# Attention of the first token pair in bursts of two tiles, beside the first sub-block's expert passes

## The chip, the cores and the metric

The kernel runs on one core of a Trainium2 chip. The metric is device microseconds of one execution. Before the change the median of three runs is 1481.53 us (1480.02 to 1481.65). Matrix products run on TensorE (PE in the profile); VectorE (DVE), ScalarE (ACT) and GpSimd (POOL) do the elementwise work, and every DMA is issued by SyncE's queue (SP). Each engine works through its own instructions in order and waits on semaphores for the others.

## The reference

Two stages follow one another. First a chunked attention over q, k, v of shape 8 x 8 heads x 576 positions x 64: the sequence is cut into chunks of 64 positions, and each chunk attends only to itself.

```
scores = q_c @ k_c^T / 8                       # 64 x 64 per chunk and head
attn   = exp(scores - max) ; attn /= (sum(attn) + 1e-9)
x      = attn @ v_c                            # back to 4608 tokens x 512
```

Then a dense mixture of four experts over those 4608 tokens, all experts for all tokens:

```
p   = domain_probs / (sum + 1e-9)
out = sum over e of  p[:, e] * (relu(x @ w1[e]) @ w2[e])      # 512 -> 1024 -> 512
```

## The kernel before

**Tiles and passes.** A tile is 128 tokens (two chunks of all eight heads), a sub-block 512 tokens, a pair two sub-blocks (eight tiles). The 4608 tokens are one first sub-block and four pairs. An expert's hidden layer is cut in halves, so each set of tokens needs eight passes, one per expert and half. The products are done in a split form: every fp32 operand is kept as a high and a low part, and each product is the sum of three partial ones (hi-hi, hi-lo, lo-hi).

**The first sub-block** goes through plain passes 0 to 7. Pass 0 is woven into the start-up. Each of passes 1 to 7 (`plain_pass`) is eight steps of 12 partial products each: four hidden steps (`plain_hidden`, f = 0 to 3), whose results go through ReLU on ACT (L721) and a low part on DVE (L722), and four output steps (`Tile.whole`, tiles 0 to 3), whose results DVE adds to the output (L1011). An output step takes its 12 products in the order f = 0 to 3, three for each f; the first six use the first half of the pass's second weights, the last six the second half.

**Weights made beside it.** While these passes run, POOL prepares weights: the low parts of the pass's second weights (`w2_split`, on POOL as L435 `hf<-wf`, `hf<-ws` or `hf<-hf`, four quarters per pass), the low parts of the next pass's first weights (`wf<-wf`), and sums and low parts of factors that later pairs will use (`acc`, `xh`, `xl`). Each low part follows a cast on ACT (L432). So the second half of a pass's output step 0, from its eighth product, needs what POOL finishes last of that pass's four quarters.

**Attention beside it.** The attention of pair 0, the eight tiles that the fast passes start with, is a generator (`attention`) that `Beside.go` moves on by one piece before each step of the plain passes; so its order is written out by hand, and a piece's instructions stand in each engine's queue just before the step's own. A tile takes five pieces: subtract the row maximum (DVE L307, L309) and exponential (ACT L312); row sums, reciprocal and scaling (DVE L315, L316, L318, L322) and a 32x32 block transpose (DVE L188); placing the blocks (ACT L194, L198, five copies); an empty piece; and the burst on PE. A burst before the change is 16 products of 64x64 for the values of the tile that is ready (L208), then 16 for the scores of the next tile (L161), each shown in the trace as two records. Scores and values lie in two halves of one PSUM tile, `psa`, and two ACT copies (L221, L222) take the values to x.

**PSUM banks.** Six banks A0, A1, B0, B1, C0, C1 are given out in rotation by `bank()`. In passes 1 to 6 all eight steps take the next one in turn. In pass 7 the four hidden steps take the next in turn, but the four output tiles have names of their own:

```
o = tiles(0, n, range(NT), ("A1", "B1", "C0", "C1") if last_pass else None)
```

**Later pairs.** Pair 1 uses the one-tile form inside the fast passes (`attend`). Pairs 2 and 3 use a two-tile form (`attend_two`): `two_next` does the values of two tiles (L282, 32 products of 64x64 into the two banks B1 and C1) and the scores of the next two (L263, 32 products into both halves of `psa`) in one burst; the second tile's q and k are loaded into columns of x's own buffer (`xraw`) that are not yet written, and its v into others. `inverse_sums` puts the row sums z into PSUM in all forms.

Of the kernel before, what the change touches and what calls it, by code (L numbers as in the profile page):

```python
# [8 lines left out]
F32 = mybir.dt.float32  # L9
# [22 lines left out]
def chunk_attention_moe(ctx: ExitStack, tc: tile.TileContext, qk, v, v0, dp, w1, w2, out):  # L32
# [33 lines left out]
    def bank(name=None):  # L66
        if name is None:
            name = BANKS[turn[0] % len(BANKS)]
            turn[0] += 1
        return ps.tile([P, SUB], F32, name=name)  # L70
# [47 lines left out]
    def a_load(t):  # L118
        s = st[t] = {}
        s["x"] = load.tile([P, 2, 2, HG, C], F32, name="qk_in")  # L120
        nc.sync.dma_start(out=s["x"], in_=qk[t].rearrange("g c d x h s -> (c d) g x h s"))

    def a_load_v(t, odd=(False, True)):
        s = st[t]
        if not odd[0]:
            s["v"] = load.tile([P, 2 * HG, C], F32, name="v_in")
        to, of = (
            a.rearrange("p (g i h) d -> p g i (h d)", g=2, i=2) for a in (s["v"], v[t - NT])
        )
        if not odd[0]:  # L130
            nc.sync.dma_start(out=to[:, :, 0], in_=of[:, :, 0])
        if odd[-1]:
            for half in range(2):
                rows, other = slice(half * C, (half + 1) * C), slice((1 - half) * C, (2 - half) * C)
                nc.sync.dma_start(out=to[rows, :, 1], in_=of[other, :, 1])

    def a_load_after(t):
        if (t + 1 - NT) % (PAIR * NT):
            a_load(t + 1)
# [23 lines left out]
    def a_less_max(t):  # L163
        less_max(st[t]["sc"])

    def a_exps(t):
        a_exp(st[t]["sc"])
# [9 lines left out]
    def a_scale(t):  # L177

        s = st[t]
        s["e"] = att.tile([P, 2, HG, C], F32, name="e")  # L180
        scale(s["e"], s["sc"], s["r"])
# [5 lines left out]
    def a_transpose(t):  # L187
        nc.vector.transpose(st[t]["sc"], st[t]["e"])  # L188

    def a_place(t, name="pt"):  # L190

        s = st[t]
        s["pt"] = att.tile([P, 2, HG, C], F32, name=name)
        nc.scalar.copy(out=s["pt"], in_=s["sc"])  # L194
        for half in range(2):
            for i in range(2):
                here, there = (slice(half * C + k * B, half * C + (k + 1) * B) for k in (i, 1 - i))
                nc.scalar.copy(  # L198
                    out=s["pt"][there, :, :, i * B : (i + 1) * B],
                    in_=s["sc"][here, :, :, (1 - i) * B : (2 - i) * B],  # L200
                )
# [31 lines left out]
    def two_load(t, i):  # L233
        if i == 0:
            a_load(t)
            return
        pair = (t - NT) // (PAIR * NT)
        to = of_tiles(pair, 6, 2).rearrange("p (g x) (h s) -> p g x h s", x=2, h=HG)
        st[t] = {"x": to}
        for g in range(2):  # L240
            nc.sync.dma_start(out=to[:, g], in_=qk[t, g].rearrange("c d x h s -> (c d) x h s"))

    def two_load_v(t, i, odd):
        if i and not odd:
            pair, j = divmod(t - NT, PAIR * NT)
            st[t]["v"] = of_tiles(pair, 7 if j == 7 else 5, 1).rearrange("p j (h d) -> p j h d", h=2)
        elif not odd:
            st[t]["v"] = load.tile([P, NK, 2, C], F32, name="v_in")
        to = st[t]["v"].rearrange("p (g i) h d -> p g i h d", i=2)
        of = v[t - NT].rearrange("p (g i h) d -> p g i h d", g=2, i=2)  # L250
        if not odd:
            nc.sync.dma_start(out=to[:, :, 0], in_=of[:, :, 0])
            return
        for half in range(2):
            rows, other = slice(half * C, (half + 1) * C), slice((1 - half) * C, (2 - half) * C)
            nc.sync.dma_start(out=to[rows, :, 1], in_=of[other, :, 1])
# [6 lines left out]
            nc.tensor.matmul(s["sc"][of_half(half), c, slot], lhsT=q, rhs=k, start=True, stop=True)  # L263

    def two_sums(t):
        z = bank("B1")[:, : 2 * HG].rearrange("p (c j) -> p c j", c=2)
        st[t]["r"] = inverse_sums(st[t]["sc"], z)

    def two_weights(t):
# [1 line left out]
        a_scale(t)  # L271
        a_transpose(t)

    def two_next(t, scores):

        av = None
        if t is not None:
            av = [bank(name).rearrange("p (i j k) -> p i j k", i=2, k=C) for name in ("B1", "C1")]
            for i in range(2):
                s = st.pop(t + i)  # L280
                for c, half, slot, head in quarters():
                    nc.tensor.matmul(  # L282
                        av[half][of_half(slot % 2), i, head // 2],
                        lhsT=s["v"][of_half(half), head // 2, head % 2],
                        rhs=s["pt"][of_half(half), c, slot], start=True, stop=True,
                    )
        if scores is not None:
            for i in range(2):
                two_scores(scores + i, i)
        if av:  # L290
            pair, j = divmod(t - NT, PAIR * NT)
            to = of_tiles(pair, j, 2).rearrange("p j (i c q) -> p i j c q", i=2, c=2)
            for half in range(2):
                for odd in range(2):
                    nc.scalar.copy(out=to[:, :, odd::2, half ^ odd], in_=av[half][:, :, odd::2])
# [25 lines left out]
    def scale(e, a, r):  # L321
        nc.vector.tensor_tensor(out=e, in0=a, in1=r, op=ALU.mult)  # L322

    def attention(pair, close):

        first = (1 + pair * PAIR) * NT
        last = first + PAIR * NT  # L330
        a_load(first)
        yield
        a_next(None, first)
        for t in range(first, last):

            if close:
                steps = (a_less_max, a_exps), (a_weights, a_transpose), (None, a_place), (None, None)
            else:
                steps = (a_less_max, a_exps), (a_sums, a_scale), (a_transpose, None), (a_place, None)
            for now, then in steps:  # L340
                yield
                if now:
                    now(t)
                if then:
                    deferred.append(lambda then=then: then(t))
            yield
            a_next(t, t + 1 if t + 1 < last else None)

    def a_next(t, after, loads=True):

        if t is not None:
            a_values(t)
        if after is not None:
            a_scores(after)

        if t is not None:
            a_copy(t)
        if loads and after is not None:
            a_load_v(after)
            a_load_after(after)  # L360

# [108 lines left out]
    class Factors:  # L472


        def __init__(self, i, n, places):
            self.i, self.n, self.made = i, n, {}
            self.at = {f"a{f + 1}{k + 1}": raw[i, f, k] for f, k in QUADS}
            self.places = places
# [436 lines left out]
    class Outer:  # L915
# [17 lines left out]
        def add(self, src, i, s):  # L933
            key = self.n // n_pass, 2 * i + self.g + NK * s
            if key not in acc:
                acc[key] = opool.tile([P, SUB], F32, name=f"acc{key[1]}")
                nc.scalar.copy(out=acc[key], in_=src)
            else:
                nc.vector.tensor_tensor(out=acc[key], in0=src, in1=acc[key], op=ALU.add)  # L939
# [337 lines left out]
    class Beside:  # L1277


        def __init__(self, pair, close):  # L1280
            self.steps = attention(pair, close)

        def go(self):
            next(self.steps, None)
# [173 lines left out]
    def loads(at, i, t):  # L1458

        for after, f in enumerate((  # L1460
            lambda: a_load_v(t, (False,)), lambda: a_load_v(t, (True,)), lambda: a_load_after(t),
        )):
            later.append((i + 2 + after, f)) if i + 2 + after >= len(WOVEN) else add(at, i + 2 + after, f)
# [4 lines left out]
    def attend(at, pair, places, i):  # L1468
        t = (1 + pair * PAIR) * NT + i
        after = t + 1 if i + 1 < PAIR * NT else None  # L1470
        if i == 0:
            add(at, 13, lambda: a_next(None, t, False))
            add(at, 14, lambda: a_softmax(t))
            loads(at, 13, t)
        add(at, places[0], lambda: a_weights(t), lambda: a_transpose(t))
        add(at, places[1], lambda: a_place(t))
        add(at, places[2], lambda: a_next(t, after, False))
        if after:
            add(at, places[2] + 1, lambda: a_softmax(after))
            loads(at, places[2], after)  # L1480
# [255 lines left out]
        by_halves(steps["b"])  # L1736

    with tc.manual_schedule():
        beside = Beside(0, True)
        startup(beside)  # L1740
        xs = []
        for n in range(1, n_pass):
            held = plain_pass(n, beside, xs)
        ahead = first_later_pass(n_pass, held)
        for n in range(n_pass + 1, n_run):
            ahead = later_pass(n, *ahead)
        last_products(ahead[0])
# [45 lines left out]
```

## Time and profile before

| quantity | value |
|---|---|
| median of three runs | 1481.53 us |
| profiled execution | 1479.55 us, span 1477.5 us |
| PE busy | 1462.5 us (99%) |
| DVE, ACT, POOL busy | 1076.6 (73%), 623.6 (42%), 980.4 us (66%) |
| DMA engines' mean busy share | 71.5% over the span, 86 to 98% from 44 to 176 us |
| granted PE clock | 1.00 |
| 64x64 products of pair 0 | from 40.8 to 162 us |

How to read it: the page gives one profiled execution. A row of the timeline has the start, the duration, the engine, the kernel line, the operation with what it writes and reads, and how many instructions were merged (x7); in square brackets stands how long the engine was idle before it and what ended that. PE's records are pipelined: in a row of equal products one starts every 0.227 us though each lasts 0.39. A product of the plain passes is one such record.

### The profile page before, as it was taken

What the parts mean: (1) busy time and instruction counts of PE and PEld (TensorE: products, weight loads), DVE (VectorE), ACT (ScalarE), POOL (GpSimd) and SP (SyncE); (2) the same over time, 40 slices, a digit from 0 to 9 for tenths busy, and PEclk for the clock granted to TensorE, in tenths of its full rate; (3) what the DMA queues carried; (4) which work ended last, traced back from release to release, by engine and by line L of the source; (5) the groups of instructions that cost most, each with busy time, mean ns of one, the idle gap of its engine ahead of it and who ended that gap; (6) DMA issues with size and microseconds to landing.
All of it is one profiled execution on the core that took longest, in us unless ns stands there. A gap on an engine that the chain in (4) does not pass through costs nothing.

```text
span 1477.5 us, 23345 instructions
## 1 busy us (share of the span) xinstructions
PE 1462.5 (99%) x8556; PEld 1199.4 (81%) x8556; DVE 1076.6 (73%) x1490; ACT 623.6 (42%) x1165; POOL 980.4 (66%) x730
## 2 busy tenths in 40 slices
PE   8999999999999999999999999999999999999998
PEld 7887877787778788888888888888888888888887
DVE  5566658888887886777766977777668866666665
ACT  4556634544454444444433434444334333333332
POOL 5778888888877785555657656555557655555555
PEclk9999999999999999999999999999999999999999
DMA  8798886878777789766665689676555696665655
GB/s 308 266 335 317 304 299 220 267 232 271 242 244 237 243 260 264 248 216 232 196 213 195 218 228 283 217 242 201 193 205 195 200 255 197 202 206 191 208 189 154
DMA packets 201250, 346.94 MB, mean 235 GB/s; under 512 B 70176, under 2 KB 114480, under 8 KB 200752
## 3 DMA queue, kind: packets, MB, share of 16 engines
q1 hardware_dynamic: 201136, 345.45, 71.5%
q8 instruction: 68, 1.11, 0.3%
q14 instruction: 46, 0.38, 0.1%
HBM read 274.01 MB, written 71.38 MB: 234 GB/s over the span
## 4 chain that ended last, share of the span: by engine, by line
PE 89%; DVE 4%; POOL 3%; issue 1%; DMA 1%; ACT 1%; SPq 0%; POOLq 0%; DVEq 0%; ACTq 0%
PE A L714 47%; PE C L714 26%; PE B L714 13%; POOL hf L435 2%; DVE acc L939 1%; PE psa L208 1%; PE psa L263 1%; PE psa L161 1%; DVE xraw L560 1%; DVE xl L435 1%; POOL wf L435 1%; POOL hf L892 1%; PE B L282 0%; DVE wraw L883 0%; DMA wf<-w 0%
## 5 line engine op out<-in xcount | busy, mean ns | idle before, releaser
L892 POOL TENSOR_TENSOR hf<-wraw,hf 128x512 fp32r<-128x512 f32 x384 | 510.1, 1347 | 222.7 <-ACT hf L889 221.3
L714 PE MATMUL A<-hf,wf 128*128 128x512 f32 x1536 | 392.9, 391 | 3.2 <-POOL hf L892 1.6
L714 PE MATMUL A<-xh,wf 128*128 128x512 f32 (+1 forms) x1104 | 380.5, 388 | 0.0
L889 ACT CAST hf<-wraw 128x512 fp32r<-128x512 f32 x384 | 234.2, 622 | 297.0 <-DVE wraw L883 96.2
L714 PEld LDWEIGHTS A<-hf,wf 128*128 128x128 f32 x1536 | 285.5, 188 | 68.4 <-DVE acc L939 5.9
L714 PEld LDWEIGHTS A<-xh,wf 128*128 128x128 f32 x1104 | 206.7, 188 | 42.9
L777 ACT COPY s<-A 128x512 f32<-128x512 f32 x192 | 112.8, 588 | 291.2 <-PE A L714 290.8
L714 PE MATMUL A<-xl,wf 128*128 128x512 f32 (+1 forms) x552 | 213.7, 388 | 0.0
L939 DVE TENSOR_TENSOR acc<-A,acc 128x512 f32<-128x512 f32 x232 | 158.0, 681 | 71.9 <-PE A L714 71.3
L714 PE MATMUL C<-xh,wf 128*128 128x512 f32 (+1 forms) x600 | 203.5, 386 | 0.7 <-ACT xh L432 0.7
L714 PE MATMUL C<-hf,wf 128*128 128x512 f32 x768 | 195.4, 390 | 1.8 <-DVE acc L939 1.7
L714 PEld LDWEIGHTS C<-hf,wf 128*128 128x128 f32 x768 | 143.8, 188 | 33.2 <-DVE acc L939 2.3
L714 PEld LDWEIGHTS C<-xh,wf 128*128 128x128 f32 x600 | 111.4, 188 | 24.1 <-ACT xh L432 0.8
L883 POOL TENSOR_TENSOR wf<-wraw,wf 128x512 f32<-128x512 f32 x31 | 40.6, 1310 | 128.9 <-DVE wf L877 128.9
L714 PE MATMUL B<-xh,wf 128*128 128x512 f32 (+1 forms) x376 | 125.1, 383 | 0.0
L892 POOL TENSOR_TENSOR hf<-wf,hf 128x512 fp32r<-128x512 f32 x64 | 90.9, 1420 | 48.8 <-ACT hf L889 48.8
L714 PEld LDWEIGHTS A<-xl,wf 128*128 128x128 f32 x552 | 103.5, 188 | 21.2
L939 DVE TENSOR_TENSOR acc<-C,acc 128x512 f32<-128x512 f32 x120 | 82.7, 689 | 45.1 <-PE C L714 42.6
L714 PE MATMUL C<-xl,wf 128*128 128x512 f32 (+1 forms) x300 | 114.5, 385 | 0.0
L883 DVE TENSOR_TENSOR wraw<-wf,wraw 128x512 f32<-128x512 f32 x64 | 95.4, 1491 | 5.2 <-POOL hf L892 4.0
L714 PE MATMUL B<-hf,wf 128*128 128x512 f32 x384 | 97.8, 390 | 0.0
L883 POOL TENSOR_TENSOR wraw<-wraw 128x512 f32<-128x512 f32 x64 | 94.2, 1472 | 0.0
(218 smaller groups left out, 1969.0 us busy)
## 6 DMA issues: line engine op xcount, KB each, us to landing
wf<-w SPq DMA_DIRECT2D x399, 512.0 KB, 4.2
w<-wf SPq DMA_DIRECT2D x49, 512.0 KB, 5.0
w<-hf SPq DMA_DIRECT2D x28, 512.0 KB, 7.4
qk_in<-in_qk SPq DMA_DIRECT2D x24, 512.0 KB, 5.8
w<-hf SPq DMA_DIRECT2D x42, 256.0 KB, 5.1
wf<-in_w SPq DMA_DIRECT2D x19, 512.0 KB, 7.1
ws<-p_t SPq DMA_DIRECT2D x24, 256.0 KB, 3.9
xraw<-in_w SPq DMA_DIRECT2D x24, 256.0 KB, 4.3
```

The source lines that it names most:

```text
L161: nc.tensor.matmul(s["sc"][of_half(half), c, slot], lhsT=q, rhs=k, start=True, stop=True)
L208: nc.tensor.matmul(av[of_half(slot % 2), half, head // 2], lhsT=s["v"][of_half(half), head], rhs=s["pt"][of_half(half), c, slot], start=Tr ...
L263: nc.tensor.matmul(s["sc"][of_half(half), c, slot], lhsT=q, rhs=k, start=True, stop=True)
L435: eng.tensor_tensor(out=t[1], in0=src, in1=t[0].bitcast(F32), op=ALU.subtract)
L560: (eng or nc.vector).tensor_tensor(out=to, in0=a, in1=b, op=op)
L714: nc.tensor.matmul(out, lhsT=lhs(k, a), rhs=rhs(k, b), start=first and i == 0, stop=last and i == len(parts) - 1, skip_group_check=not (fi ...
L777: nc.scalar.copy(out=t, in_=self.a)
L883: (eng or nc.vector).tensor_tensor(out=self.values[place, k], in0=self.values[a, k], in1=self.values[b, k], op=op)
L889: nc.scalar.copy(out=self.part(name, 0)[:, k], in_=self.values[name, k])
L892: (eng or nc.gpsimd).tensor_tensor(out=self.part(name, 1)[:, k], in0=self.values[name, k], in1=self.part(name, 0)[:, k].bitcast(F32), op=A ...
L939: nc.vector.tensor_tensor(out=acc[key], in0=src, in1=acc[key], op=ALU.add)
```

## The change

The generator for pair 0 now takes tiles two by two. It loads two tiles at first, does the scores of both in one burst, then runs the same five pieces for the one and for the other, and after the tenth piece calls `two_next`: values of both, scores of the next two, four ACT copies (L295). So nine bursts become five. The pieces on DVE and ACT keep their places. `two_next` gets an argument for its banks; pair 0 passes (None, None), so the values of two tiles take the next two banks of the rotation. The second tile's q and k come in two DMAs into columns of x (L241 in place of L121), its v into other columns. The row sums z of the two-tile form move from PSUM (bank B1) to a small SBUF tile `zs`; that also holds for pairs 2 and 3. `a_next` loses an argument that pair 1 always gave as False.

```diff
     def two_sums(t):
-        z = bank("B1")[:, : 2 * HG].rearrange("p (c j) -> p c j", c=2)
+        z = small.tile([P, 2, HG], F32, name="zs")
         st[t]["r"] = inverse_sums(st[t]["sc"], z)
...
-    def two_next(t, scores):
+    def two_next(t, scores, banks=("B1", "C1")):
         av = None
         if t is not None:
-            av = [bank(name).rearrange("p (i j k) -> p i j k", i=2, k=C) for name in ("B1", "C1")]
+            av = [bank(name).rearrange("p (i j k) -> p i j k", i=2, k=C) for name in banks]
...
-    def attention(pair, close):
+    def attention(pair):
         first = (1 + pair * PAIR) * NT
         last = first + PAIR * NT
-        a_load(first)
+        def loads(t, i):
+            for odd in (False, True):
+                two_load_v(t, i, odd)
+            if t + 2 < last:
+                two_load(t + 2, i)
+
+        for i in range(2):
+            two_load(first + i, i)
         yield
-        a_next(None, first)
-        for t in range(first, last):
-            if close:
-                steps = (a_less_max, a_exps), (a_weights, a_transpose), (None, a_place), (None, None)
-            else:
-                steps = (a_less_max, a_exps), (a_sums, a_scale), (a_transpose, None), (a_place, None)
-            for now, then in steps:
+        two_next(None, first)
+        for t in range(first, last, 2):
+            loads(t, 0)
+            for i in range(2):
+                u = t + i
                 yield
-                if now:
-                    now(t)
-                if then:
-                    deferred.append(lambda then=then: then(t))
-            yield
-            a_next(t, t + 1 if t + 1 < last else None)
+                a_less_max(u)
+                deferred.append(lambda u=u: a_exps(u))
+                yield
+                two_sums(u)
+                a_scale(u)
+                deferred.append(lambda u=u: a_transpose(u))
+                yield
+                deferred.append(lambda u=u, i=i: a_place(u, ("pt", "e")[i]))
+                yield
+                yield
+                if i == 0:
+                    loads(t + 1, 1)
+            two_next(t, t + 2 if t + 2 < last else None, (None, None))
...
-        beside = Beside(0, True)
+        beside = Beside(0)
```

The line numbers of the kernel after are six higher from `a_next` on (L714 becomes L720, L435 L441, L722 L728). Three places in the instruction order matter for what follows.

PE, the first burst (between output tiles 2 and 3 of pass 0) and the place between the hidden steps and output step 0 of pass 1, before. The names are the banks and `psa`, each with a number for the allocation.

```order
L714 MATMUL C1_704<-hf5_470,hf1_358 128x512 x2
L161 MATMUL psa_95<-qk_in_600 64x64 x16
L714 MATMUL A1_740<-hf4_449,hf0_343 128x512 x4
...
L714 MATMUL B1_836<-xh0_236,wf2_696 128x512
L208 MATMUL psa_95<-pt_830,v_in_734 64x64 x16
L161 MATMUL psa_95<-qk_in_738 64x64 x16
L714 MATMUL C0_899<-hf4_774,hf0_757 128x512 x6
```

The same two places after:

```order
L720 MATMUL C1_707<-hf5_470,hf1_358 128x512 x2
L263 MATMUL psa_95<-qk_in_600 64x64 x16
L263 MATMUL psa_95<-xraw_602 64x64 x16
L720 MATMUL A1_759<-hf4_449,hf0_343 128x512 x4
...
L720 MATMUL B1_856<-xh0_236,wf2_699 128x512
L720 MATMUL C0_883<-hf4_793,hf0_776 128x512 x6
```

The first burst has doubled; the second is gone, and output step 0 follows the last hidden step directly. The values of tiles 0 and 1 come five steps later, with the scores of tiles 2 and 3.

PE, pass 7, from the end of hidden step f = 3 to output tile 1, before:

```order
L714 MATMUL C1_2395<-xl0_237,wf2_2267 128x512
L714 MATMUL C1_2395<-xh0_236,wf2_2267 128x512
L714 MATMUL A1_2417<-hf4_2335,hf0_2319 128x512 x6
L714 MATMUL A1_2417<-hf5_2358,hf1_2367 128x512 x6
L714 MATMUL B1_2440<-hf4_2335,hf0_2319 128x512 x6
```

PE at the same place after the change:

```order
L720 MATMUL A1_2407<-xl0_237,wf2_2279 128x512
L720 MATMUL A1_2407<-xh0_236,wf2_2279 128x512
L720 MATMUL A1_2429<-hf4_2347,hf0_2331 128x512 x6
L720 MATMUL A1_2429<-hf5_2370,hf1_2379 128x512 x6
L720 MATMUL B1_2452<-hf4_2347,hf0_2331 128x512 x6
```

Four bursts with two banks each have turned the rotation by eight, that is by two of six: the hidden step f = 3 writes A1 where it wrote C1, and output tile 0, which has A1 by name, follows it in the same bank.

DVE, the softmax of the first tile of pair 0, before (`z4` is the reciprocal, `e` the scaled weights):

```order
L315 TENSOR_REDUCE psa_95<-psa_95 128x8
L316 TENSOR_SCALAR psa_95<-psa_95 128x8
L318 RECIPROCAL z4_785<-psa_95 128x8
L322 TENSOR_TENSOR e_787<-psa_95,z4_785 128x512
L722 SCALAR_TENSOR_TENSOR hf0_757<-A1_789,hf0_757 128x512
```

The same rows of DVE after the change:

```order
L315 TENSOR_REDUCE zs_802<-psa_95 128x8
L316 TENSOR_SCALAR zs_802<-zs_802 128x8
L318 RECIPROCAL z4_805<-zs_802 128x8
L322 TENSOR_TENSOR e_807<-psa_95,z4_805 128x512
L728 SCALAR_TENSOR_TENSOR hf0_776<-A1_809,hf0_776 128x512
```

The sequence is the same on DVE throughout; only the place of the eight sums has moved. POOL's sequence has not changed at all.

More of the change, by code (lines that the diff above doesn't have):

```diff
@@ L322, in scale, with a_next @@
         nc.vector.tensor_tensor(out=e, in0=a, in1=r, op=ALU.mult)
-    def attention(pair, close):
+    def attention(pair):
         first = (1 + pair * PAIR) * NT
         last = first + PAIR * NT
-        a_load(first)
-        yield
-        a_next(None, first)
-        for t in range(first, last):
-            if close:
-                steps = (a_less_max, a_exps), (a_weights, a_transpose), (None, a_place), (None, None)
-            else:
-                steps = (a_less_max, a_exps), (a_sums, a_scale), (a_transpose, None), (a_place, None)
-            for now, then in steps:
-                yield
-                if now:
-                    now(t)
-                if then:
-                    deferred.append(lambda then=then: then(t))
-            yield
-            a_next(t, t + 1 if t + 1 < last else None)
-    def a_next(t, after, loads=True):
+        def loads(t, i):
[5 more added lines that the diff above has]
+            two_load(first + i, i)
+        yield
+        two_next(None, first)
[3 more added lines that the diff above has]
+                u = t + i
+                yield
+                a_less_max(u)
[11 more added lines that the diff above has]
+            two_next(t, t + 2 if t + 2 < last else None, (None, None))
+    def a_next(t, after):
         if t is not None:
@@ L357, in a_next @@
             a_copy(t)
-        if loads and after is not None:
-            a_load_v(after)
-            a_load_after(after)
     KEYS = {"a11": 0, "a12": 1, "a22": 2, "s1": 3, "s2": 4, "s3": 5, "s4": 6}
@@ L1277, in chunk_attention_moe, with __init__ @@
     class Beside:
-        def __init__(self, pair, close):
-            self.steps = attention(pair, close)
+        def __init__(self, pair):
+            self.steps = attention(pair)
         def go(self):
@@ L1471, in attend @@
         if i == 0:
-            add(at, 13, lambda: a_next(None, t, False))
+            add(at, 13, lambda: a_next(None, t))
             add(at, 14, lambda: a_softmax(t))
@@ L1476, in attend @@
         add(at, places[1], lambda: a_place(t))
-        add(at, places[2], lambda: a_next(t, after, False))
+        add(at, places[2], lambda: a_next(t, after))
         if after:
```

## The prediction

> **What bounds the kernel now.** I read the page first, then the timeline of PE from 40 to 205 us, where pair 0's attention runs, then those of POOL, ACT and DVE over the same stretch, to see what ends each wait of PE there.
>
> ```profile
> PE 1462.5 (99%) x8556; PEld 1199.4 (81%) x8556; DVE 1076.6 (73%) x1490; ACT 623.6 (42%) x1165; POOL 980.4 (66%) x730
> PE 89%; DVE 4%; POOL 3%; issue 1%; DMA 1%; ACT 1%; SPq 0%; POOLq 0%; DVEq 0%; ACTq 0%
> ```
>
> PE is busy for 99% of the span and 89% of the chain that ended last is PE's. So time taken from PE counts, unless PE then waits for something that did not move with it. In the plain passes there is such a thing:
>
> ```profile
> 110.47 2.55 POOL L435 TENSOR_TENSOR wf<-wf,wf 128x512 fp32r<-128x512 f32 x2 [3.16 <-ACT wf L432]
> 125.17 5.02 POOL L435 TENSOR_TENSOR hf<-hf,hf 128x512 fp32r<-128x512 f32 x4
> 127.92 1.75 PE L714 MATMUL A<-hf,hf 128*128 128x512 f32 x7
> 130.24 0.97 PE L714 MATMUL A<-hf,hf 128*128 128x512 f32 x3 [0.58 <-POOL hf L435]
> ```
>
> In pass 4, output step 0 issues seven products and stops before the eighth, the first that needs POOL's last quarter of the second weights. POOL ends it at 125.17 + 5.02 = 130.19, PE goes on at 130.24. POOL had worked without a pause since 110.47.
>
> **What the bursts cost.** A burst of one tile, then one of two tiles from a later pair, each with the ordinary products around it:
>
> ```profile
> 100.28 0.39 PE L714 MATMUL B<-xh,wf 128*128 128x512 f32 x1
> 100.63 0.69 PE L208 MATMUL psa<-pt,v_in 64*64 64x64 f32 x32
> 101.78 0.50 PE L714 MATMUL B<-xh,wf 128*128 128x512 f32 x1
> 102.12 0.39 PE L714 MATMUL B<-xl,wf 128*128 128x512 f32 x1
> 102.35 0.62 PE L714 MATMUL B<-xh,wf 128*128 128x512 f32 x2
> ...
> 612.18 0.39 PE L714 MATMUL C<-xh,wf 128*128 128x512 f32 x1
> 612.50 0.27 PE L282 MATMUL B<-pt,v_in 64*64 64x64 f32 x1
> 614.58 1.19 PE L714 MATMUL A<-hf,wf 128*128 128x512 f32 x4
> ```
>
> An ordinary step is 0.23 us (102.12 to 102.35), but the way in takes 0.32 to 0.35 and the first step after it 0.34. So the one-tile burst costs 102.12 - 100.28 - 2 x 0.23 = 1.38 us, the two-tile one 614.58 - 612.18 + 0.34 - 2 x 0.23 = 2.28. Seven one-tile bursts lie between these two rows:
>
> ```profile
> 55.44 0.69 PE L208 MATMUL psa<-pt,v_in 64*64 64x64 f32 x32
> 146.61 0.69 PE L208 MATMUL psa<-pt,v_in 64*64 64x64 f32 x32
> ```
>
> The same subtraction gives 1.45, 1.35, 1.23, 1.38, 1.46, 1.35 and 1.39 for them, 9.6 in all. The first burst (scores alone) and the last (values alone), and the same two of a later pair:
>
> ```profile
> 40.83 0.74 PE L161 MATMUL psa<-qk_in 64*64 64x64 f32 x32
> 41.50 0.72 PE L714 MATMUL A<-hf,hf 128*128 128x512 f32 x2
> 161.67 0.69 PE L208 MATMUL psa<-pt,v_in 64*64 64x64 f32 x32
> 162.30 0.73 PE L714 MATMUL C<-hf,hf 128*128 128x512 f32 x2
> ...
> 572.72 0.39 PE L714 MATMUL C<-xh,wf 128*128 128x512 f32 x1
> 574.18 1.19 PE L714 MATMUL A<-hf,wf 128*128 128x512 f32 x4
> 733.48 0.39 PE L714 MATMUL C<-xh,wf 128*128 128x512 f32 x1
> 734.89 1.43 PE L714 MATMUL A<-hf,wf 128*128 128x512 f32 x5
> ```
>
> With 0.32 for the way in and 0.34 - 2 x 0.23 = -0.12 for the rest, the scores alone cost 0.87 now and 1.34 then, the values alone 0.83 and 1.29. Nine bursts cost 0.87 + 9.6 + 0.83 = 11.3, five will cost 1.34 + 3 x 2.28 + 1.29 = 9.5. PE is given 1.8 us. That alone would be 0.12%.
>
> **Where the 1.8 us go.** I follow PE's shift against the run before (minus is earlier). After the first burst +0.47; where the burst at 55 us stood -0.98; after 70 us (2.28 for 1.35) -0.05; after 85 us -1.28; after 100 us -0.38; after 115 us -1.84. So PE would reach output step 0 of pass 4 1.84 us earlier. But POOL's run that ends at 130.19 starts from an earlier point of PE:
>
> ```profile
> 104.83 0.60 ACT L721 ACTIVATE hf<-B 128x512 fp32r<-128x512 f32 x1 [1.93 <-PE B L714]
> 109.28 0.58 ACT L312 ACTIVATE psa<-psa 128x512 f32<-128x512 f32 x1 [3.34 <-DVE psa L309]
> ```
>
> Hidden step f = 3 of pass 3 (shift -0.38) releases ACT at 104.83, that releases DVE's ReLU part, a weight sum and the row maximum queued behind it, those the exponential at 109.28, and the casts behind the exponential start POOL at 110.47. The change moves none of these on ACT, DVE or POOL, so POOL ends 0.38 earlier and PE goes on with -0.38: 1.46 us of the gain become a longer wait. The burst at 131 us then costs 0.93 more: +0.55. In pass 5 it repeats:
>
> ```profile
> 143.95 0.60 ACT L721 ACTIVATE hf<-C 128x512 fp32r<-128x512 f32 x1 [2.39 <-PE C L714]
> 147.28 2.55 POOL L435 TENSOR_TENSOR hf<-acc,hf 128x512 fp32r<-128x512 f32 x2 [2.14 <-ACT hf L432]
> 152.29 2.54 POOL L435 TENSOR_TENSOR hf<-ws,hf 128x512 fp32r<-128x512 f32 x2
> 153.33 2.98 PE L714 MATMUL B<-hf,hf 128*128 128x512 f32 x12
> ```
>
> POOL's run starts from hidden step f = 0 of pass 5 (143.95, shift +0.55), by way of the placing copies and casts on ACT, and ends at 154.83; the eighth product of output step 0 is due at 153.33 + 7 x 0.227 = 154.92, with 0.1 us to spare. The burst that disappears at 146.6 lies between the two, so its 1.39 us are a wait again: +0.5. The last burst adds 0.46: +1.0. In pass 6 PE and POOL both follow hidden step f = 0, and the shift stays.
>
> **The bank.** In pass 7:
>
> ```profile
> 194.57 6.03 POOL L435 TENSOR_TENSOR hf<-wf,hf 128x512 fp32r<-128x512 f32 x4
> 198.18 1.75 PE L714 MATMUL A<-hf,hf 128*128 128x512 f32 x7
> 199.90 0.69 DVE L722 SCALAR_TENSOR_TENSOR hf<-C,hf 128x512 fp32r<-128x512 f32 x1 [1.78 <-ACT hf L721]
> 200.65 1.43 PE L714 MATMUL A<-hf,hf 128*128 128x512 f32 x5 [0.73 <-POOL hf L435]
> ```
>
> Today output tile 0 issues seven products into A1 while the hidden result f = 3 in C1 is still read by ACT and DVE, and waits for POOL until 200.65. Afterwards f = 3 is in A1 itself, and DVE leaves it at 199.90 + 0.69 = 200.59, as late as POOL's end. So all twelve products come after 200.65 and not five: 7 x 0.227 = +1.6. No work is left to hide them; behind them on PE stand tiles 1 to 3 and the first fast pass, whose first waits are ended by results that follow PE's own products, so I let the shift pass through. Sum: +1.0 + 1.6 = +2.6 us on the profiled 1479.55. The median shown is 2.0 above that execution, so I add it there: 1481.5 + 2.6 = 1484.1.
>
> **The parts I cost at nothing.** Four copies instead of two on ACT after a burst add 0.7 us, and ACT has idle stretches of 1.9 us (before 104.83) and 2.4 (before 143.95). Three more DMA issues at each second tile, and loads into x's columns, come about 15 us before the burst that needs them. The values' two banks are next used four or more steps (11 us) later. The sums in SBUF:
>
> ```profile
> L316 DVE TENSOR_SCALAR psa<-psa x20: 174/174/175, 8.7 to 447.4; 128x8 f32<-128x8 f32 x20
> 26.42 1.30 POOL L486 TENSOR_TENSOR acc<-hf 128x512 f32<-128x512 f32 x1
> 27.27 0.49 DVE L78 TENSOR_SCALAR prs<-prs 128x36 f32<-128x36 f32 x1
> ```
>
> In PSUM the small addition takes 174 ns every time. The only one from SBUF to SBUF takes 0.49 us, and ends at 27.76, just when POOL's instruction ends (27.72). So the price per tile lies between -0.17 (free) and one POOL instruction, +1.3, by the row it is nearest to +0.3. I take zero for the path, since the softmax is ahead of what waits for it; least where casts on ACT stand behind a placing and POOL needs them:
>
> ```profile
> 116.73 0.61 ACT L432 CAST xl<-xh 128x512 fp32r<-128x512 f32 x1
> 117.63 1.29 POOL L435 TENSOR_TENSOR xl<-xh,xl 128x512 fp32r<-128x512 f32 x1
> ```
>
> There, in POOL's run before pass 4's output step 0, the cast ends at 117.34 and POOL reads it at 117.63: 0.3 us to spare. The Trainium skill (SBUF — State Buffer, section "Who interferes with whom") says that a tensor_scalar in a two-port mode takes a port pair that it shares with GpSimd as an exclusive lock, so that the later of the two blocks fully; the two ends above agree with it. By that rule the addition can lose a whole POOL instruction, which is the third rival.
>
> **Rivals.** (1) The burst saving arrives whole, 1481.5 - 1.8 = 1479.7. For it: PE's 99%. Against it: the two POOL runs above, which start before the bursts that vanish. It needs POOL's runs to move with PE and the bank to be free early. 0.08. (2) The bank costs nothing more than POOL's wait did, because ACT, which is held before f = 3 by casts, comes to it earlier: +1.0, 1482.5. Against it: those casts have no earlier trigger. 0.18. (3) Slower beyond doubt: the sums in SBUF wait behind POOL. At 111 us POOL runs (from 110.47 on); if the softmax of that tile comes 1.3 us later, the casts behind its placing reach POOL 1.0 us late (0.3 to spare), pass 4's output step 0 waits that much longer, and nothing later gives it back: +3.6, 1485.1. It decides from 0.3 us of delay on. 0.22. (4) The two-tile burst itself waits, for the second tile's placing: its place in ACT's queue is the same as before, where the waits ahead of the seven bursts sum to 0.3 us (their costs differ by no more), so this moves little; I count it with the forecast, 0.52.
>
> **Numbers.** What a measurement of this kernel can tell from no change is about 0.2%, 3.0 us. The forecast, +2.6, is inside that, with an uncertainty of about 1 us from the three waits, so a third of its chance (0.18) and most of (3) (0.20) lie beyond: slower 0.38. Of (1) a third, with 0.02 for what I have not seen, lies on the other side: faster 0.05. Same 0.57. The likeliest time is 1484.1, its own range 1482.8 to 1485.4; with (2) and (3) and part of (1) the range is 1480.3 to 1486.4.
>
> **What would show it.** Five bursts between 40 and 165 us, the middle three 2.3 us long. In passes 4 and 5 output step 0 stops before its eighth product for some 2.2 and 1.4 us, by POOL. In pass 7 its twelve products stand together after a wait for DVE's `hf` at L728, and PE from there on is about 2.6 us later than before. If those twelve come within 0.3 us of the hidden step's end, the bank step is wrong; if pass 4 has no longer wait than now, the POOL step is; if L316 on `zs` takes over 0.5 us and the casts are late, rival 3 has come.

## The result, and the profile after

The kernel after takes 1486.96 us (median of six, 1486.36 to 1488.33), the kernel before 1480.92 in the same session: a ratio of 1.0044, interval 1.0034 to 1.0054. The change costs 6.0 us. The forecast was 1484.1 (+2.6), with a range that ended at 1486.4. The profiled execution took 1487.81 us, 8.3 more than the one of before.

The page of the kernel after, busy time and chain of waits:

```profile
PE 1465.2 (99%) x8556; PEld 1199.7 (81%) x8556; DVE 1090.5 (73%) x1490; ACT 623.4 (42%) x1165; POOL 979.1 (66%) x730
PE 84%; DVE 7%; POOL 4%; ACT 2%; issue 1%; DMA 1%; SPq 0%; ACTq 0%; POOLq 0%; DVEq 0%
```

PE is as busy as before, but the chain now runs through DVE for 7% and not 4%, and DVE is busy for 14 us more, with the same 1490 instructions. The waits of PE from 30 to 300 us (engine, what it wrote, what ended the wait: sum in us, count, longest), without two rows of 1.6 and 0.5 us that the kernel before has as well:

```profile
PE A L720 <- DVE hf L728: 2.2, 1, 2.2
PE A L720 <- issue: 1.8, 2, 1.0
PE C L720 <- POOL hf L441: 1.8, 2, 1.0
PE B L720 <- POOL hf L441: 1.3, 1, 1.3
```

The POOL rows and the DVE row are the waits that the prediction named. The second row is new: twice PE stood still for nothing that the profile shows.

Both kernels issue the same 6198 products of the plain line (L714, now L720) in the same order, so they can be laid side by side, product by product. The difference of their start times is PE's shift:

| place on PE | forecast | after | all three causes removed (below) |
|---|---|---|---|
| after the first burst (41 us) | +0.5 | +0.45 | -0.07 |
| where the burst at 55 us stood | -1.0 | -0.88 | -1.41 |
| after the burst at 70 us | -0.1 | -0.09 | -0.61 |
| where the burst at 85 us stood | -1.3 | -1.41 | -1.93 |
| after the burst at 100 us | -0.4 | -0.53, at once +0.40 | -1.06 |
| pass 4, output step 0, eighth product | -0.4 | +0.50 | -0.65 |
| after the burst at 131 us | +0.55 | +1.42, then +2.60 | +0.28 |
| pass 5, output step 0, eighth product | +0.5 | +3.18 | +0.71 |
| after the last burst (162 us) | +1.0 | +3.69 | +1.22 |
| pass 7, behind output tile 0 | +2.6 | +6.70 | +1.2 |
| last product (1472 us) | +2.6 | +8.86 | +1.38 |

(In the last column PE's first product of the passes came 0.54 us earlier than in the kernel before; that start varies by up to 1 us between the runs.) The arithmetic of the bursts holds to 0.1 or 0.2 us at each place up to the burst at 100 us; from there on the new waits are mixed in. A two-tile burst in the timeline after, its first rows and the two behind it:

```profile
98.85 0.39 PE L720 MATMUL C<-xh,wf 128*128 128x512 f32 x1
99.17 0.27 PE L282 MATMUL C<-pt,v_in 64*64 64x64 f32 x1
...
101.25 0.50 PE L720 MATMUL A<-xh,wf 128*128 128x512 f32 x1
101.58 0.40 PE L720 MATMUL A<-xl,wf 128*128 128x512 f32 x1
102.75 0.51 PE L720 MATMUL A<-xh,wf 128*128 128x512 f32 x1 [0.77 <-issue]
```

By the prediction's subtraction it costs 101.58 - 98.85 - 2 x 0.23 = 2.27 us (predicted 2.28). Then comes the new wait: the next product starts 1.17 us later instead of 0.23. The second such wait stands after the burst at 132 us (137.06 in place of 135.88, 1.2 lost).

The last large step is in pass 7, and the last 2.1 us come in six steps of 0.34, three in pair 2 and three in pair 3. Both are read below, where the runs tell what they are.

### The profile page after: what moved, and what is told of

Its sections match the earlier page's. It is cut to its first block, busy times and chain, and to the rows that moved or that the text cites. A ratio compares the mean times of both kernels' runs of the same rounds, so it can differ in the third digit from the quotient of the medians.

```text
span 1485.8 us, 23360 instructions
## 1 busy us (share of the span) xinstructions
PE 1465.2 (99%) x8556; PEld 1199.7 (81%) x8556; DVE 1090.5 (73%) x1490; ACT 623.4 (42%) x1165; POOL 979.1 (66%) x730
## 3 DMA queue, kind: packets, MB, share of 16 engines
q8 instruction: 68, 1.11, 0.3%
## 4 chain that ended last, share of the span: by engine, by line
PE 84%; DVE 7%; POOL 4%; ACT 2%; issue 1%; DMA 1%; SPq 0%; ACTq 0%; POOLq 0%; DVEq 0%
PE A L720 45%; PE C L720 23%; PE B L720 13%; POOL hf L441 2%; DVE acc L945 1%; PE psa L263 1%; DVE xraw L566 1%; DVE wraw L889 1%; POOL wf L441 1%; ACT pt L198 1%; PE B L282 1%; DVE xl L441 1%; POOL hf L898 1%; ACT hf L895 1%; DVE m L307 0%
## 5 line engine op out<-in xcount | busy, mean ns | idle before, releaser
L720 PE MATMUL A<-hf,wf 128*128 128x512 f32 x1536 | 393.7, 392 | 3.6 <-POOL hf L898 1.6
L720 PE MATMUL A<-xh,wf 128*128 128x512 f32 (+1 forms) x1128 | 388.4, 388 | 0.8 <-issue 0.8
L720 PEld LDWEIGHTS A<-hf,wf 128*128 128x128 f32 x1536 | 285.2, 188 | 70.7 <-DVE acc L945 8.8
L720 PEld LDWEIGHTS A<-xh,wf 128*128 128x128 f32 x1128 | 211.2, 188 | 44.8 <-issue 1.2
L720 PE MATMUL A<-xl,wf 128*128 128x512 f32 (+1 forms) x564 | 218.4, 388 | 0.0
L720 PE MATMUL C<-xh,wf 128*128 128x512 f32 (+1 forms) x600 | 203.8, 387 | 0.7 <-ACT xh L438 0.7
L720 PE MATMUL C<-hf,wf 128*128 128x512 f32 x768 | 195.4, 390 | 1.9 <-DVE acc L945 1.7
L720 PEld LDWEIGHTS C<-hf,wf 128*128 128x128 f32 x768 | 143.9, 188 | 33.3 <-DVE acc L945 2.3
L720 PEld LDWEIGHTS C<-xh,wf 128*128 128x128 f32 x600 | 111.5, 188 | 24.1 <-ACT xh L438 0.8
L720 PEld LDWEIGHTS A<-xl,wf 128*128 128x128 f32 x564 | 105.8, 188 | 21.8
L720 PE MATMUL B<-xh,wf 128*128 128x512 f32 (+1 forms) x352 | 116.8, 382 | 0.0
L720 PE MATMUL C<-xl,wf 128*128 128x512 f32 (+1 forms) x300 | 114.5, 385 | 0.0
L720 PE MATMUL B<-hf,wf 128*128 128x512 f32 x384 | 97.8, 390 | 0.0
```

The source lines that it names most:

```text
L720: nc.tensor.matmul(out, lhsT=lhs(k, a), rhs=rhs(k, b), start=first and i == 0, stop=last and i == len(parts) - 1, skip_group_check=not (fi ...
```

## The experiments

By this trace my theory was that three things had come on top of the forecast: the two unnamed waits (PE's instruction code), the bank of pass 7 with a clock penalty, and the sums in SBUF in pairs 2 and 3. The first four runs take them one at a time.

### The sums of pairs 2 and 3

```
 def two_sums(t):
-    z = small.tile([P, 2, HG], F32, name="zs")
+    if t >= (1 + PAIR) * NT:
+        z = bank("B1")[:, : 2 * HG].rearrange("p (c j) -> p c j", c=2)
+    else:
+        z = small.tile([P, 2, HG], F32, name="zs")
```

> The kernel after, with the row sums of pairs 2 and 3 back in PSUM (bank B1); pair 0 keeps them in SBUF. Theory: in the kernel after each of those small additions that meets a POOL instruction lasts until that instruction ends (0.58 us in six of sixteen, against 0.17), the placing behind it comes 0.4 us later, and through DVE's queue a bank is given back late: PE loses 0.34 us in each of the six passes. Then the six steps at 638, 679, 720, 954, 995 and 1035 us vanish, and the time is 1486.96 - 2.0 = 1485.0. Rival: the six steps come from elsewhere in pairs 2 and 3 (later phase of the passes against POOL), and the time stays at 1487.0.

Measured: 1486.19 us, ratio 1.0034 (1.0022 to 1.0046). The line of the small addition in the kernel after (shortest, median and longest duration in ns):

```profile
L316 DVE TENSOR_SCALAR zs<-zs x24: 171/583/1335, 49.7 to 1049.5; 128x8 f32<-128x8 f32 x24
```

Its 24 instructions in pairs 0, 2 and 3 took 174 or 175 ns before. One of them in pair 2, in the timeline of DVE, POOL and PE:

```profile
629.79 0.59 DVE L316 TENSOR_SCALAR zs<-zs 128x8 f32<-128x8 f32 x1
...
627.81 2.55 POOL L898 TENSOR_TENSOR hf<-wraw,hf 128x512 fp32r<-128x512 f32 x2 [5.60 <-ACT hf L895]
...
636.43 1.52 PE L720 MATMUL B<-hf,wf 128*128 128x512 f32 x6
638.03 1.65 PE L720 MATMUL A<-hf,wf 128*128 128x512 f32 x6
```

The addition ends at 630.38, POOL's instruction at 630.36. It is so with 16 of the 24 additions (eight in pair 0, eight in pairs 2 and 3): each takes 0.5 us or more and ends 0.03 us behind a POOL instruction. The other eight take 0.17; two of them meet no POOL instruction, and six start in the last 0.13 us of one. From there DVE runs 0.4 us late through the scaling, the transpose, ACT's placing and the next tile's maximum, gives a bank back late, and at 638.03 PE starts 1.60 us behind the step before instead of 1.37. The same line and the same products in the run with the sums in PSUM:

```profile
L319 DVE TENSOR_SCALAR B<-B x16: 174/175/175, 588.5 to 1048.4; 128x8 f32<-128x8 f32 x16
```

```profile
637.36 1.53 PE L723 MATMUL B<-hf,wf 128*128 128x512 f32 x6
638.73 1.54 PE L723 MATMUL A<-hf,wf 128*128 128x512 f32 x6
```

All six steps are gone; behind pass 7 the shift no longer grows. The mechanism is settled. The median fell by 0.8 only. In the profiled execution the unnamed wait at 102 us cost 1.54 us, 0.6 more than in the kernel after; of the others that is not known. The price by the median is left to the later runs.

### The bank of pass 7

```
-            two_next(t, t + 2 if t + 2 < last else None, (None, None))
+            more = t + 2 < last
+            ahead = [BANKS[(turn[0] + k) % len(BANKS)] for k in (2, 3)]
+            two_next(t, t + 2 if more else None, (None, None) if more else ahead)
```

> The kernel after, with the last burst of pair 0 writing two banks by name (those two and three steps ahead in the rotation) instead of the next two, so the rotation is turned by six and pass 7 has the banks of the kernel before. Theory: hidden step f = 3 of pass 7 is in C1 again, output tile 0 starts at once, stops before its eighth product for POOL for 0.8 us, and the eight products at half rate behind the 2.2 us wait are at full rate. PE is 3.0 us earlier from there on: 1484.0. Rival A: the half rate is not a consequence of the wait and stays, so that 1.4 are won: 1485.6. Rival B: the bank costs nothing, since POOL ends at the same time: 1487.0.

Measured: 1485.61 us, ratio 1.0037 (1.0024 to 1.0049). Pass 7 in the timeline of the kernel after, PE and the DVE instruction that it waits for:

```profile
201.62 0.39 PE L720 MATMUL A<-xh,wf 128*128 128x512 f32 x1
204.20 4.54 PE L720 MATMUL A<-hf,hf 128*128 128x512 f32 x12 [2.18 <-DVE hf L728]
...
203.45 0.69 DVE L728 SCALAR_TENSOR_TENSOR hf<-A,hf 128x512 fp32r<-128x512 f32 x1 [1.78 <-ACT hf L727]
```

And three windows there, ahead of the wait, behind it and after. A row has the window, its length, the busy time and number of instructions of PE, PE's weight loads, DVE, ACT and POOL, then the granted clock (PEclk, third from the end), the DMA share and GB/s:

```profile
200.50:201.70 1.20, 1.20 (x7) 0.93 (x5) 0.69 (x1) 1.20 (x3) 1.20 (x2) 1.00 1.05 406
204.20:207.60 3.40, 3.40 (x8) 2.72 (x9) 2.18 (x1) 1.09 (x2) 3.40 (x3) 0.51 0.93 287
207.60:211.00 3.40, 3.40 (x16) 2.77 (x16) 2.22 (x2) 0.00 (x0) 3.40 (x3) 1.00 0.99 398
```

Twelve products stand together after a wait for DVE, as predicted. What was not predicted: for 3.4 us after the wait PE has half its clock, 8 products in 3.40 us where 16 fit. The same place of PE with the rotation turned back:

```profile
204.19 1.75 PE L722 MATMUL A<-hf,hf 128*128 128x512 f32 x7
206.64 1.20 PE L722 MATMUL A<-hf,hf 128*128 128x512 f32 x4 [0.70 <-POOL hf L443]
```

The seven products come first again and the shift is the same behind the tile as before it (+6.0). Rival B has fallen. The median is the one that rival A gave, but not for its reason: the half clock has left pass 7. This execution had lost 3.5 us elsewhere, at the first unnamed wait, in its timeline and in the window behind it:

```profile
103.33 0.73 PE L722 MATMUL A<-xh,wf 128*128 128x512 f32 x2 [1.59 <-issue]
```

```profile
103.30:107.00 3.70, 3.67 (x10) 2.97 (x11) 0.00 (x0) 0.00 (x0) 1.17 (x1) 0.61 1.03 384
```

There the wait is longer (1.76 us lost), and the half clock follows it. So the half clock belongs to a wait of PE, not to pass 7.

### The code of PE

```
         keep_warm(WAITS["softmax"])
+        for _ in range(60):
+            nc.tensor.matmul(idle[:32, :32], lhsT=zeros[:32, :32], rhs=zeros[:32, :32], start=True, stop=True)
```

> The kernel after, with 60 products of 32x32 (120 instructions, in PE's idle time near 8.3 us) put into the start-up. Nothing else moves; every later PE instruction stands 120 places later in the code. Theory: the two waits of 1.0 us at 102 and 136 us, for nothing that the profile names, are waits for PE's code: it is fetched in blocks of 16 KB (256 instructions), a two-tile burst is 256 instructions long, and where a burst starts just before a block's end (6 and 16 instructions here), PE is through the next block before it has come. With the shift all three middle bursts start some 40 to 60 instructions behind a block's start, both waits vanish, and the time is 1486.96 - 2.1 = 1484.9. Rival: they are waits for data whose DMA lands late; they stay, 1487.0.

Measured: 1486.26 us, ratio 1.0039 (1.0026 to 1.0051). The reasoning starts from the page's DMA queues and from the queues in three stretches of the kernel after (queue: packets, MB, share): the whole run, 72.6 to 100.4 us, and 100.4 to 101.6:

```profile
q8 instruction: 68, 1.11, 0.3%
...
q1 hardware_dynamic: 4684, 8.70, 93.7%
...
q8 instruction: 1, 0.02, 5.0%
```

Queue q8 moves 68 blocks of 16 KB. PE has 2 x 8556 records and 1.11 MB divided by that is 65 bytes, so I take it that q8 carries PE's code, some 256 instructions to a block. From 72.6 to 100.4 us no block starts; one starts at 100.53, in the middle of the burst, is there at 101.50, and PE goes on at 102.75. At the second wait the block comes from 134.55 to 135.62 and PE goes on at 137.06. A two-tile burst is 128 pairs of weight load and product, so it uses up one whole block in 2.2 us, where the ordinary steps take 29 us. Counted by records, both waits stand at the same instruction modulo 256 (193). If a block ends there, the two bursts begin some 6 and 16 instructions before a block's end, and the middle burst that has no wait behind it, at 69.40, begins just behind one. The burst at 100 us also begins just as ACT ends the placing that it waits for (97.67 + 1.50 = 99.17), so PE could not run ahead of it. The timeline with the code shifted:

```profile
101.00 0.39 PE L720 MATMUL A<-xl,wf 128*128 128x512 f32 x1
101.23 0.63 PE L720 MATMUL A<-xh,wf 128*128 128x512 f32 x2
```

No wait, here or after the second burst. By the count above the bursts now begin 105 to 122 instructions behind a block's start, and not 40 to 60, which is as far from its end as the theory needs. The theory's rows came true and the rival (late data) fell; the median moved by 0.7 and not 2.1. In the profiled execution 1.1 us went back at 566 us in one wait for a DMA; whether the other executions had such a thing is not known.

### The bank alone, in the kernel before

```
         at, last_pass = {}, n == n_pass - 1
+        if n in (3, 5):
+            turn[0] += 1
```

> The kernel before, with the bank rotation turned on by one in pass 3 and by one in pass 5, and nothing else: hidden step f = 3 of pass 7 comes into A1, where output tile 0 follows. Theory: output tile 0 waits 2.3 us for DVE at L722 and then runs for 3.4 us at half the clock: 1.5 + 1.6 = 3.1 us more, 1484.0. Rival (the forecast's step as it stood): 1.6 us more and the full clock, 1482.5.

Measured: 1482.22 us (1480.63 to 1484.39), ratio 1.0014 (1.0005 to 1.0023). The window of the wait and the one behind it:

```profile
198.20:200.70 2.50, 0.16 (x1) 0.00 (x0) 0.69 (x1) 2.50 (x4) 2.50 (x3) 0.94 1.02 407
200.70:204.20 3.50, 3.48 (x9) 2.79 (x10) 1.99 (x1) 1.12 (x2) 3.50 (x3) 0.56 0.93 244
```

Both readings were half right: the median is the rival's, and the theory's 3 us come in part of the executions. Of eleven executions five have a mean clock of 0.997 or 0.998 and take 1483.6 to 1484.4 us; six have 1.000 and take 1480.6 to 1482.2. So the half clock comes in some executions only and costs about 2.2 us where it comes; without it the bank costs some 1.0 us by these medians.

### All three together, and then one left in at a time

The single repairs had won 0.8, 1.4 and 0.7 us against the median of after (by the ratios to the kernel before 1.5, 1.0 and 0.7, each uncertain by about 2 us), which is less than the traces promised. The run with all three repairs asks whether they add up.

> The kernel after with the three edits of the runs before together: sums of pairs 2 and 3 in PSUM, last burst's banks by name, code shifted by 120 instructions. Theory: what the run with the shifted code showed up to pass 6 stays (PE 1.2 to 1.8 us later than in the kernel before: the burst arithmetic and the two POOL waits), and nothing is added in pass 7 nor in pairs 2 and 3. 1480.5 + 1.5 = 1482.0, so 5 us less than after. Rival: the losses do not add up, since each that is removed is replaced by another (as the single runs won only 0.7 to 1.4 each): 1485 or more.

Measured: 1480.73 us, ratio 1.0003 (0.9994 to 1.0012): the whole loss is gone. Its waits of PE from 30 to 300 us:

```profile
PE C L725 <- POOL hf L446: 2.2, 2, 1.2
PE B L725 <- POOL hf L446: 1.3, 1, 1.3
PE A L725 <- POOL hf L446: 0.7, 1, 0.7
```

What is left, beside the two rows that the kernel before has as well, are the POOL waits of passes 4, 5 and 7, two of them foreseen and one as before. Next, three runs each with two of the repairs, and the kernel after once more on the same chip.

> Sums of pairs 2 and 3 in PSUM and last burst's banks by name, but the code not shifted: only the two waits for code are left of the three losses. Theory: the run with all three plus the two waits (0.9 to 1.8 us each in the traces so far): 1480.7 + 2.5 = 1483.2; PE waits for nothing that the profile names at 102 and 136 us, and for nothing new behind. Rival (not additive, one loss hides another): within 1 us of 1480.7.

> Sums of pairs 2 and 3 in PSUM and code shifted, but the last burst's banks from the rotation: only the bank of pass 7 is left. Theory: 1.5 us in executions at a mean clock of 1.000 and 3 to 4 us in those with a stretch at half the clock (0.997 or 0.998), as in the kernel before with the rotation turned: median 1480.7 + 1.9 = 1482.6. Rival: within 1 us of 1480.7.

> Last burst's banks by name and code shifted, but all sums in SBUF: only the additions that wait for POOL in pairs 2 and 3 are left. Theory: six steps of 0.34 us on PE, 1480.7 + 2.0 = 1482.7. Rival: within 1 us of 1480.7.

> The kernel after unchanged, beside the three runs that leave one loss in. Theory: all three losses, 1480.7 + 2.5 + 1.9 + 2.0 = 1487.1. Rival: if the losses hide one another, the three runs that leave one in do not sum to it.

| left in | median us | ratio to before | above the run with all three repairs |
|---|---|---|---|
| code | 1483.60 | 1.0021 (1.0012 to 1.0030) | 2.8 |
| bank | 1482.90 | 1.0016 (1.0007 to 1.0025) | 2.1 |
| sums | 1483.09 | 1.0016 (1.0007 to 1.0025) | 2.3 |
| all (kernel after) | 1486.80 | 1.0046 (1.0033 to 1.0058) | 6.0 |

The last column is the distance from the kernel before on the same chip, less the 0.4 of the run with all three. The three sum to 7.2 where all together cost 6.0 (by the ratios 2.7 + 1.9 + 1.9 = 6.5 against 6.4). The three first runs, each with two losses left in, lie 4.6 to 5.3 above it by the ratios, where sums of two give 3.8 to 4.6. Each of these is uncertain by about 1.3 us or more, so the losses add up as far as this can tell, and the rival that they hide one another is not needed.

Two of the prices hold more than their name says. With the bank left in, two of eleven executions have a mean clock of 0.998 and eight have 1.000; the median of these eight is 1482.7, so the half clock makes no more than 0.2 of the 2.1. With the code left in, the trace has 2.6 us more than with all three up to 162 us and another 1.1 behind that, part of it a wait of 0.7 for a DMA at 600 us; how much of this the other executions have is not known.

The waits of PE from 95 to 150 us where the code is left as it was:

```profile
PE C L725 <- POOL hf L446: 2.2, 2, 1.3
PE A L725 <- issue: 2.0, 2, 1.5
```

In the five traces of kernels with two-tile bursts and unshifted code the two waits cost 0.9 to 1.8 us (first) and 0.7 to 1.2 (second); in the six with the code shifted (two of them in the next section) there is none.

### Without the addition, and with POOL's work moved

```
         nc.vector.tensor_reduce(out=z, in_=a, op=ALU.add, axis=AX)
-        nc.vector.tensor_scalar_add(z, z, 1e-9)
```

> As the run with all three, but the sums stay in SBUF and the small addition of 1e-9 is left out in every softmax (the sums are at least 1, where 1e-9 is below the last digit). Theory: pair 0's additions, which last 0.5 to 1.06 us in SBUF, are not on the path, so this equals the run with all three within 0.5 us: 1482.0. Rival: they delay placings and casts in passes 1 to 5, and leaving them out wins 1 us or more: 1481.0.

Measured: 1479.20 us, ratio 0.9993 (0.9984 to 1.0002), 1.5 less than with all three. But not where the rival put it: between 41 and 162 us PE's shift grows by 1.27 here and by 1.29 with the addition in, at the same places. Pair 0's slow additions (0.5 to 1.06 us) cost PE nothing. The gain is in the start-up, where PE is 0.2 us further ahead by 23 us (and a start that varies), and in pair 1, where PE gains 0.21, 0.33 and 0.23 us at three places (343, 379 and 425 us) where it waits for DVE's `acc`.

```
 3: [
-    (5, early_sum(last_w1, "s3")), (6, early_sum(last_w1, "s4")),
 4: [
+    (5, early_sum(last_w1, "s3")), (5, early_sum(last_w1, "s4")),
```

> As the run without the addition, and two sums of POOL (s3 and s4 of the last pass's first weights, L492, 1.30 + 1.75 us) moved from the end of pass 3 to output step 1 of pass 4, behind the second weights' low parts, where POOL is idle for 6 us before its next work. Theory: POOL's run ends 3.05 us earlier, and PE's waits in output step 0 of pass 4 (1.1 us after the first product, 0.7 us before the eighth) go: 1.8 us less than without the move, 1480.2. Rival: PE is then held by something else at once (casts on ACT, the placing): under 0.5 us less.

Measured: 1477.68 us, ratio 0.9983 (0.9974 to 0.9992). In pass 4, output step 0 on PE and the run of POOL ahead of it:

```profile
124.87 1.75 PE L721 MATMUL C<-hf,hf 128*128 128x512 f32 x7
127.20 1.42 PE L721 MATMUL C<-hf,hf 128*128 128x512 f32 x5 [0.58 <-POOL hf L442]
...
114.63 1.30 POOL L442 TENSOR_TENSOR xl<-xh,xl 128x512 fp32r<-128x512 f32 x1 [1.89 <-DMA w<-hf]
```

The wait after the first product is gone and the one before the eighth is as short as in the kernel before; the trace gains 1.9 us there, the median 1.5. The rest of the wait stays because POOL's run now pauses for a DMA before 114.63.

> The kernel before without the addition and with the same two sums of POOL moved; bursts, banks and code otherwise as before. Theory: the wait of 0.58 us before the eighth product goes and the rest stays, 0.6 us less: 1479.9. So the move is worth three times as much to the two-tile bursts as to the one-tile ones. Rival: it is worth the same to both.

Measured: 1477.94 us, ratio 0.9985 (0.9976 to 0.9994). The twelve products of that step now come in one piece:

```profile
127.29 2.88 PE L713 MATMUL A<-hf,hf 128*128 128x512 f32 x12
```

That is 0.86 us of PE's time by the shift, against 1.9 for the two-tile bursts, so the move is worth about twice as much to these and not three times; the rest of the 2.4 us is put down to the addition, which was not left out alone in this kernel. These last two kernels are the fastest of all, 2.7 and 2.4 us below the kernel before, and do not differ from each other: with every loss repaired, bursts of two tiles are worth as much as bursts of one.

## Why the prediction was wrong

**The bursts: right.** Five bursts, the middle three 2.27 us; nine cost 11.3 and five 9.4, as worked out to 0.1.

**POOL eats the gain: right, and a little short.** Pass 4 and pass 5 of the kernel after, POOL and PE:

```profile
125.66 5.03 POOL L441 TENSOR_TENSOR hf<-hf,hf 128x512 fp32r<-128x512 f32 x4
126.92 0.39 PE L720 MATMUL C<-hf,hf 128*128 128x512 f32 x1
128.26 1.66 PE L720 MATMUL C<-hf,hf 128*128 128x512 f32 x6 [0.96 <-POOL hf L441]
130.74 0.96 PE L720 MATMUL C<-hf,hf 128*128 128x512 f32 x3 [0.82 <-POOL hf L441]
...
155.02 3.02 POOL L441 TENSOR_TENSOR hf<-ws,hf 128x512 fp32r<-128x512 f32 x2
154.67 2.14 PE L720 MATMUL B<-hf,hf 128*128 128x512 f32 x7
158.10 1.65 PE L720 MATMUL B<-hf,hf 128*128 128x512 f32 x6 [1.29 <-POOL hf L441]
```

By the shift PE loses 1.50 us in pass 4 (from -1.00 to +0.50; predicted 1.46), most of it behind the first product, where the forecast had all of it at the eighth. In pass 5 it loses 1.88 (from +1.34 to +3.22; predicted 1.39): POOL's last two low parts took 3.02 us there and 2.54 before. With all three repairs, where no code wait has moved PE before pass 4, the two losses are 1.91 and 1.87. PE is then at +1.22 + 0.54 = +1.8 behind the last burst by the trace, where the forecast said +1.0, and the median says +0.4. So the sum up to here was right within what the medians can tell, and each of the two terms about 0.45 us short in the traces.

**The bank: the mechanism right, and the price where the clock stays whole.** With the bank alone left in, all twelve products of output tile 0 come behind the wait for DVE, at full clock in this execution:

```profile
202.38 3.03 PE L723 MATMUL A<-hf,hf 128*128 128x512 f32 x12 [2.12 <-DVE hf L731]
```

The shift goes from +1.92 to +3.34 there, 1.42 us (predicted 1.6). By the medians of the executions at a mean clock of 1.000 the bank costs 1.0 in the kernel before and 1.9 here. The term left out is the half clock. It adds 1.6 us in the traces that have it, but it comes in part of the executions, and the median of after is no different with it or without: the three of its six executions at 1.000 took 1486.68 to 1486.97. So the bank is not where the forecast failed.

**"The parts I cost at nothing": wrong, and this step carries the miss.** It held two of the three losses. For the sums in SBUF the prediction had the right bounds (-0.17 to +1.3 per addition), the right nearest row, +0.3 (measured 0.41 to 0.43 for six of the eight in pairs 2 and 3 that wait), and then took zero for the path, "since the softmax is ahead of what waits for it". It looked at pair 0 alone, where zero is right, and not at pairs 2 and 3, which the change touches as well. There the late softmax gives a bank back late that PE is waiting for: six times 0.34 us, 2.3 by the median. The third rival named the cause but put it in the wrong place: in pass 4 POOL's run of 19.7 us starts 0.53 later than before, as PE's own shift of +0.51 at the step that releases it has it, and is no longer than before. The bursts were also costed as time on PE alone. That 128 weight loads and 128 products must be fetched as code was in no row that I had read, though queue q8 stands on the page: 2.8 us by the median, 2.6 of it in the trace at these waits and what they shift.

So the forecast's 1.0 + 1.6 became, by the medians, 0.4 for the bursts and POOL, 2.1 for the bank, and 2.3 + 2.8 for two things that were put at nothing. These sum to 7.6, where the kernel after lies 6.4 above the kernel before on the same chip; the difference is within their uncertainty.

## What to carry to other kernels

Follow an edit to every place that it touches, not only to the one it is named for: the cheap line that was shared with pairs 2 and 3 cost about 2 us, nearly as much as the whole forecast of +2.6. Before a small vector instruction is moved from PSUM to SBUF, look at what POOL does at that time. When work on PE is put into denser bursts, count its instructions too: a burst as long as a block of code depends on where the block ends, and any edit ahead of it can move that.

## What the runs showed that I had not expected

**PE can wait for its own code.** A burst of 256 instructions in 2.2 us, begun some 6 or 16 instructions before a block's end, was followed by a wait that cost 0.7 to 1.8 us, ten times in five traces; 120 instructions more in the start-up removed it. The Trainium skill (Runtime: NRT & Kernel Launch, section "Instruction fetch mechanics") says that code is refilled in 16 KiB blocks of 256 instructions, which agrees with q8's 68 blocks, and that the fetch is mostly hidden because issue is slower than the refill; here it was not hidden. That the fetch was asked for late because PE's sequencer stood at the burst's wait is argued from one row, and was not tested.

**Behind a wait of 1.6 to 2.4 us PE can have half its clock for 3.4 us.** Six of the traces have such a stretch, behind waits of 1.59 (the run with the last burst's banks), 2.18 and 2.16 (after, twice), 2.22 (sums of pairs 2 and 3), 2.25 (shifted code) and 2.36 us (the bank alone). It did not come after 2.12 us with the bank alone left in, nor after the 1.7 to 1.95 us that PE waits near 10 us in six traces, the kernel before among them, nor in six of eleven executions of the bank alone. What decides is not shown. The Trainium skill (TensorE: Matmul & The Clock Gate, "What's actually happening") gives a free-running window of about 3.4 us; the length of the slow stretch and its coming in some executions only agree with that, while an idle time well below 3.4 us was enough.

**DVE and POOL hold each other up in SBUF, in both directions.** The small additions waited for one POOL instruction each. One full-size addition of DVE, from SBUF to SBUF, took 1.38 us before and 6.59 us in the kernel after (128.35 to 134.94), where POOL worked beside it without a pause until 134.39. No product of PE waited for that one. In the run with all three repairs the same addition got through in 1.62 us, and the POOL instruction behind it took 1.73 where its neighbours take 1.30:

```profile
126.79 1.62 DVE L497 TENSOR_TENSOR acc<-hf 128x512 f32<-128x512 f32 x1
127.81 1.73 POOL L446 TENSOR_TENSOR hf<-hf,hf 128x512 fp32r<-128x512 f32 x1
```

For that one PE does wait, in pass 4. In pass 5 of the kernel after, a POOL instruction of 1.78 us (from 156.27) has a DVE addition of two SBUF operands beside its start in the same way. That the additions are the cause there is read from these rows; no run moves them.
